# x^T U of two pairs in fp32 in four column groups, batch 1 in double pairs, and one fixed program order

## The chip, the cores and the metric

The kernel runs on one core of a Trainium2 chip. The core has five engines that work side by side and meet through semaphores: TensorE (matmul, and its weight loads), VectorE, ScalarE, GpSimd (POOL in the profile) and SyncE (SP), which here only issues DMAs. A time is the device time of one execution in microseconds; where one time is given for a kernel it is the median of its runs.

## What is computed

Linear attention, an RMS norm, and then a token-mixing and a channel-mixing layer on its output. The batch has 8 elements (called batches below), each with 8 heads, 576 positions and 64 columns a head, so x has 576 rows and 512 columns for each batch.

```python
kv = np.einsum('bhsd,bhse->bhde', k, v)
out = np.einsum('bhsd,bhde->bhse', q, kv)
rms = np.sqrt(np.mean(out * out, axis=-1, keepdims=True) + 1e-06)
attn = out / rms * g_norm                 # -> x, heads side by side
xt = x.transpose(0, 2, 1)
h = xt @ U @ V                            # U 576x32, V 32x576
u = x + h.transpose(0, 2, 1)
out = u + np.maximum(u @ w_ch1, 0.0) @ w_ch2   # 512 -> 2048 -> 512
```

## The kernel before

**Precision.** The large matmuls run in fp32r on numbers that are split in a high and a low part (hi and lo), three matmuls for each product. Small ones run in plain fp32, which TensorE does in two passes: one matmul of the program is two records in the trace.

**The channel layer.** The 8 x 576 rows of u are handled as nine blocks of 512 rows (j in the code). Blocks 0 to 2 go through `ffn1` and `ffn2` directly, 16 chunks of the 2048 columns each. Blocks 3 to 8 are taken in twos with a seven-product scheme (`product`, `product2`), whose sums and differences of u (`forms_of_u`), h (`form_of_h`) and of the weights (`sums_of_w`) VectorE and ScalarE make. The weights arrive packed and are decoded chunk by chunk during the first block (`decode_w`: a copy on ScalarE, a bit operation on VectorE, a cast on ScalarE, a subtraction on VectorE), then partly copied to DRAM (`copy_of_w`).

**The attention.** Two heads are a pair; a batch has four pairs, and two pairs are a double pair. For batches 2 to 7 a double pair is done together (`duo_tasks`): `run_step` multiplies q by K^T V for both pairs in 64-by-64 matmuls, does the tails, and in the same burst K^T V of the next double pair (`kv_double`, two column groups of 64); then squares, sums and the root (`sq`, `red`, `root`, `rms`) and the multiplications that write x (`mula`, `mulb`) follow. x is kept in `x_duo`, nine chunks of 128 columns, of which chunk 4 holds the 64 last rows of both pairs. For x^T U each pair's x is then cast to its high part (`xsplit_step`, ScalarE), the low part is made by two subtractions (`low_parts`, VectorE, into `st`), and nine fp32r matmuls of 64 weight columns (hi and lo of U side by side in `u2`) add up (`t_step`). `t4_step` builds the four-strip stationary matrix from the result, `mix_step` multiplies it by V, and `add_step` adds it to the transposed x, which takes the way of VectorE's 32-by-32 transpose and DRAM (`turn`, `out`, `in`). `into_blocks` (`g`) scales by g and splits u into its hi and lo blocks.

Batch 1 is done pair by pair instead (`pair_tasks`): an output step of five fp32 matmuls (`out_step`), x^T U in plain fp32 with 96 weight columns for pairs 0 to 2 and in the split form for pair 3 (`T32`), and K^T V as a burst of its own. Batch 0 is the start-up: it has its own steps and its own plan.

**What sets the order.** From block 0 on each step has a place, a number, in the tables (`DUOS`, `PAIRS`, `FORMSAT`, `FINISH`, `PREP`, ...). A place counts groups of twelve large matmuls: block j < 3 has places 32j to 32j + 32, one for each `ffn1` or `ffn2` chunk. `do` emits the steps whose place has been reached, between two groups of matmuls. In block 0 the emitted order binds only in part: TensorE keeps it from chunk 13 on (`PIN0`), VectorE, ScalarE and SP from place 32 on (`ORDERED`); before that a scheduler places the instructions. The q loads, the stores of the output (`finish`, with the places in `FINISH`) and the transposes' DMAs all go through SP's queue, which keeps its order.

Of the kernel before, what the change touches and what calls it, by code (L numbers as in the profile page):

```python
# [10 lines left out]
F32 = mybir.dt.float32  # L11
# [27 lines left out]
T32 = ('ffff', 'fffr')  # L39
SSQ = ('vvvv', 'vvvv', 'vvvv')  # L40
MULS = ('vvvv', 'vvvv')
STEPS = ('kv', 'kvl', 'out', 'ql', 'split', 'turn', 't', 'mix')
REST = {0: 1, 1: 47.15, 2: 77.8, 4: 113.1, 6: 167.4}
RESTLOAD = {1: 41.6, 2: 67.15, 4: 104.4, 6: 161.6}
FORMSAT = {3: ((89, 89.16, 89.27, 91.33, 91.34, 91.6, 91.61, 91.87, 92.8, 93.4, 93.85), (96, 96.26, 96.47, 97.13, 97.19, 97.95, 98.56, 99.12, 99.23, 100.54, 101.4)), 5: ((143.9, 144.21, 144.22, 147.58, 149.64, 149.8, 150.21, 151.37, 151.53, 151.95, 152.4), (149.1, 150.41, 151.97, 153.23, 153.44, 153.7, 154.56, 154.92, 155.63, 156.24, 157.3)), 7: ((194.35, 194.46, 195.47, 197.88, 200.79, 204.2, 204.31, 204.62, 204.83, 205.74, 207.4), (206.8, 207.81, 207.97, 208.58, 209.54, 209.7, 209.71, 210.17, 210.73, 211.24, 212.55))}
# [3 lines left out]
FOLLOW = {  # L49
# [22 lines left out]
PIN0 = 13  # L72
# [16 lines left out]
def build(ctx: ExitStack, tc: tile.TileContext, kv0_in, kv_in, q_in, uv_in, w_in, out):  # L89
# [20 lines left out]
    u2 = const.tile([P, NT, 2 * R], F32R, name="u2")  # L110
# [397 lines left out]
    def xsplit_step(b, p, late=False):  # L508

        s = state[b, p]  # L510
        xh = sc.tile([P, NT, P], F32R, name="xh")
        xl = st.tile([P, 4, P], F32R, name=f"st{p % 2}")
        n = p if b == 0 else -1
        move("xh", n, xh, s["x"])
        s["hl"] = (xh, xl)
        if not late:
            low_parts(s)

    def low_parts(s):

        xh, xl = s["hl"]
        n = -1
        tail = s.get("tail", 4)
        main, own = (slice(0, 4), slice(0, TAIL)) if tail else (slice(1, NT), slice(TAIL, P))
# [659 lines left out]
```

## Time and profile before

| | us |
|---|---|
| median of 3 runs (lowest, highest) | 837.23 (836.54, 837.96) |
| the profiled execution | 836.27 |
| its span | 834.5 |
| TensorE busy | 821.4 |
| VectorE busy | 590.5 |
| ScalarE busy | 362.8 |

The span is the time from the first to the last instruction of the profiled execution. Busy time is a union: a matmul's record lasts longer than its share of the stream, because matmuls are pipelined, so records overlap, and what one costs is read from the starts of its neighbours. An idle time in brackets behind a row names what ended it.

### The profile page before, as it was taken

Reading aid. Unit: us, or ns where it says so; the run is one execution under the profiler, and the core shown is the slowest. Engines: PE = TensorE matmul, PEld = TensorE weight load, DVE = VectorE, ACT = ScalarE, POOL = GpSimd, SP = SyncE. Lnnn points to the kernel's source line nnn. Section 1 sums busy time; section 2 is a strip of 40 time slices with the busy share of each in tenths; the row PEclk is TensorE's granted clock in tenths of the full one; section 3 lists DMA queues with packets and bytes.
Section 4 is the critical chain, followed back from the end, with each engine's and each line's share of the span. In section 5 each row is a group of like instructions: output and inputs, shape, how many; then the busy total and the mean of one; then the engine's idle time right before and its main releaser. Section 6 shows DMA issues by size and latency. Waiting matters only on the chain.

```text
span 834.5 us, 13626 instructions
## 1 busy us (share of the span) xinstructions
PE 821.4 (98%) x5157; PEld 681.5 (82%) x5157; DVE 590.5 (71%) x895; ACT 362.8 (43%) x615; POOL 8.3 (1%) x37
## 2 busy tenths in 40 slices
PE   8999998999999999999999999999999999999998
PEld 7788887788888788888888888888888888888886
DVE  4887655768889765849956798578557983862385
ACT  4766431333333432446535454554255445322531
POOL 3000000000000000000000000000000000000000
PEclk9999999999999999999999999999999999999999
DMA  9996767555679452879688689768667686666665
GB/s 351 382 367 245 271 235 256 184 194 166 215 218 302 154 173 85 270 258 309 223 262 272 204 273 298 258 221 239 225 182 234 209 281 196 175 201 199 198 200 176
DMA packets 109840, 195.33 MB, mean 234 GB/s; under 512 B 10832, under 2 KB 45904, under 8 KB 107984
## 3 DMA queue, kind: packets, MB, share of 16 engines
q1 hardware_dynamic: 109632, 194.33, 71.2%
q8 instruction: 41, 0.67, 0.4%
q14 instruction: 23, 0.19, 0.1%
q10 hardware_dynamic: 144, 0.13, 0.0%
HBM read 145.14 MB, written 49.28 MB: 233 GB/s over the span
## 4 chain that ended last, share of the span: by engine, by line
PE 89%; DVE 6%; ACT 2%; DMA 1%; issue 1%; SPq 0%; DVEq 0%; ACTq 0%
PE y L140 67%; PE h L140 14%; PE pt L140 4%; PE ph L140 3%; PE pp L140 3%; DVE dec L130 2%; DVE st L130 1%; DMA uvs<-uv_in 1%; DVE hhl L130 1%; DVE ss L130 1%; DVE x L130 0%; DVE h L130 0%; DMA ut<-q_in 0%; ACT hhl L130 0%; DVE ta L130 0%
## 5 line engine op out<-in xcount | busy, mean ns | idle before, releaser
L140 PE MATMUL y<-entry,ring 128*128 128x512 f32 x576 | 135.5, 390 | 0.0
L140 PE MATMUL y<-hhl,ws 128*128 128x512 f32 x540 | 132.3, 392 | 0.0
L140 PEld LDWEIGHTS y<-entry,ring 128*128 128x128 f32 x576 | 107.6, 188 | 22.3 <-DVE entry L130 0.2
L140 PE MATMUL h<-uth,ws 128*128 128x512 f32 x360 | 119.8, 393 | 0.5 <-DVE hhl L130 0.2
L140 PEld LDWEIGHTS y<-hhl,ws 128*128 128x128 f32 x540 | 99.7, 188 | 20.3 <-ACT hhl L130 0.2
L130 DVE TENSOR_TENSOR h<-y,h 128x512 f32<-128x512 f32 x71 | 48.1, 685 | 59.4 <-PE y L140 59.1
L140 PE MATMUL y<-uB,ringw 128*128 128x512 f32 x354 | 85.2, 390 | 0.0
L140 PE MATMUL y<-uT,ring 128*128 128x512 f32 x348 | 82.9, 390 | 0.0
L140 PEld LDWEIGHTS h<-uth,ws 128*128 128x128 f32 x360 | 67.6, 188 | 16.2 <-DVE hhl L130 1.7
L130 ACT ACTIVATE hhl<-h 128x512 fp32r<-128x512 f32 (+1 forms) x53 | 34.4, 648 | 101.6 <-PE h L140 86.2
L140 PEld LDWEIGHTS y<-uB,ringw 128*128 128x128 f32 x354 | 66.1, 188 | 13.8 <-issue 0.2
L140 PEld LDWEIGHTS y<-uT,ring 128*128 128x128 f32 x348 | 65.0, 188 | 13.4
L130 ACT COPY h<-y 128x512 f32<-128x512 f32 x70 | 40.6, 585 | 80.3 <-PE y L140 80.0
L130 DVE TENSOR_TENSOR entry<-h,entry 128x1024 fp32r<-128x1024 f32 x48 | 58.1, 1218 | 21.0 <-ACT entry L130 20.9
L140 PE MATMUL h<-utl,ws 128*128 128x512 f32 x180 | 70.4, 391 | 0.0
L130 DVE SCALAR_TENSOR_TENSOR hhl<-h,hhl 128x512 fp32r<-128x512 f32 (+1 forms) x53 | 39.6, 747 | 41.7 <-ACT hhl L130 41.6
L130 ACT CAST entry<-h 128x1024 fp32r<-128x1024 f32 x48 | 49.8, 1051 | 35.7 <-PE y L140 30.1
L140 PE MATMUL y<-entry,ringw 128*128 128x512 f32 x216 | 55.2, 391 | 0.0
L140 PE MATMUL y<-hhl,ringw 128*128 128x512 f32 x216 | 54.9, 390 | 0.0
L140 PE MATMUL y<-uT,ringw 128*128 128x512 f32 x210 | 50.8, 390 | 0.0
L140 PEld LDWEIGHTS y<-hhl,ringw 128*128 128x128 f32 x216 | 40.5, 188 | 8.7 <-ACT uth L130 0.3
L140 PEld LDWEIGHTS y<-entry,ringw 128*128 128x128 f32 x216 | 40.1, 188 | 8.2 <-DVE entry L130 0.2
(206 smaller groups left out, 1111.3 us busy)
## 6 DMA issues: line engine op xcount, KB each, us to landing
ring<-wd SPq DMA_DIRECT2D x69, 256.0 KB, 3.5
kv_sb<-kv_in SPq DMA_DIRECT2D x14, 1216.0 KB, 7.0
ringw<-wd SPq DMA_DIRECT2D x66, 256.0 KB, 3.4
raw<-w_in SPq DMA_DIRECT2D x30, 511.8 KB, 10.2
ring<-w1s SPq DMA_DIRECT2D x48, 256.0 KB, 3.7
ringw<-w1s SPq DMA_DIRECT2D x48, 256.0 KB, 3.5
ring<-w2s SPq DMA_DIRECT2D x48, 256.0 KB, 4.2
ringw<-w2s SPq DMA_DIRECT2D x48, 256.0 KB, 4.3
```

The source lines that it names most:

```text
L130: ins = getattr(self.eng, name)(*args, **kw)
L140: ins = nc.tensor.matmul(*args, **kw)
```

## The change

x^T U of a double pair becomes one step (`t_both`): ten fp32 matmuls take x straight from `x_duo` with 32 weight columns each, in four column groups (two halves of the sum for each pair), so that no high and low parts of x are needed. `t_sums` adds the halves (a ScalarE copy, a VectorE addition), `t4_late` builds the stationary matrix from the sum; `u1` holds U in fp32 and is filled on POOL. Batch 1 is done in double pairs like the others, with K^T V of its first one at place 6.15. Program order binds on all engines from block 0 on, and the decoding of chunks 3 to 15 gets places of its own (`DECODE`, four parts each). All tables have new numbers; of the ones cut below the numbers alone differ. Some buffers change: `xt` has one for each pair of a double pair, the forms of u and the outputs use `st0` to `st3`, and the forms of u come in another order.

```diff
-T32 = ('ffff', 'fffr')
+T32 = ('ffff',)
...
-FINISH = {0: (33.5, 34.5, 33.15, 33.3), 1: (65.55, 67.85, 66.2, 66.3), 2: (97.7, 97.85, 98.65, 101.5)}
-ORDERED = 32
+REST = {0: 8.45, 1: 50.95, 2: 85.35, 4: 113.2, 6: 160.3}
+RESTLOAD = {1: 45.05, 2: 79.45, 4: 103.6, 6: 157.7}
...
+FINISH = {0: (33.95, 37.7, 37.15, 36.75), 1: (65.96, 65.09, 66.75, 69.65), 2: (98.95, 99.85, 97.9, 100.25)}
+DECODE = ((2.36, 2.77, 2.78, 3.73), (3.34, 3.89, 4.49, 4.64), (4.45, 5.4, 5.8, 6.2), (5.41, 6.21, 7.61, 8.31), (7.07, 8.52, 9.72, 10.37), (10.38, 10.43, 10.73, 10.98), (12.4, 12.54, 12.59, 12.69), (13.4, 13.55, 13.95, 14.15), (14.26, 16.71, 16.91, 17.91), (17.27, 18.77, 20.82, 21.52), (20.98, 22.03, 22.88, 23.93), (22.39, 24.29, 25.59, 25.84), (25.35, 25.9, 26.1, 26.45))
...
-FIRSTKV = 28
-GROUPS = ('kvl', 'ql', 'run', 'sq', 'kvc', 'red', 'root', 'rms', 'mula', 'mulb', 'casta', 'suba', 'turna', 'outa', 'ina', 'ta', 't4a', 'mixa', 'adda', 'ga', 'castb', 'subb', 'turnb', 'outb', 'inb', 'tb', 't4b', 'mixb', 'addb', 'gb')
+FIRSTKV = 6.15
+GROUPS = ('kvl', 'ql', 'run', 'sq', 'kvc', 'red', 'root', 'rms', 'mula', 'mulb', 't', 'ts', 'turna', 'outa', 'ina', 'turnb', 'outb', 'inb', 't4a', 'mixa', 'adda', 'ga', 't4b', 'mixb', 'addb', 'gb')
...
-    2: ((50.5, 33.95, 35.05, 35.1, 39.55, 35.2, 35.4, 35.45, 35.55, 37.65, 36.35, 36.4, 35.8, 37.05, 38.1, 38.3, 38.6, 39.2, 40.7, 43.3, 38.55, 39.2, 38.35, 38.55, 40.4, 40.45, 41.05, 41.1, 41.3, 46.35), (32.5, 32.4, 42.6, 42.85, 52.55, 43.1, 43.25, 43.35, 43.4, 46.05, 44.75, 46.7, 46.95, 47.3, 50.25, 48.9, 51.15, 52.8, 52.9, 55, 49.75, 51.1, 51.95, 52.3, 54.15, 52, 52.1, 54.9, 55.75, 57.4)),
...
+    1: ((4.45, 10.4, 12.8, 13.2, 14.5, 13.45, 13.65, 13.75, 14.2, 14.6, 17, 18.6, 15.9, 18.85, 20, 15.55, 21.4, 24.85, 21.55, 23.3, 24.7, 25.44, 19.6, 25.1, 26.45, 26.75), (11.3, 12.9, 19.23, 19.34, 20.31, 19.65, 20.31, 20.47, 20.83, 21.92, 24.26, 25.17, 23.94, 25.75, 26.05, 22.18, 25.25, 26, 26.48, 28.09, 29.45, 31.45, 28.94, 29.85, 29.95, 31.45)),
+    2: ((14.12, 27, 31.15, 32.6, 36.4, 33.2, 33.6, 34.15, 34.85, 35.45, 39.3, 39.45, 35.5, 36.65, 38.95, 37.65, 38.9, 40.85, 39.75, 40.2, 40.6, 47.25, 40.7, 41, 42.35, 44.5), (20.95, 32.25, 43.4, 44.55, 50.15, 44.7, 45.15, 45.55, 46.05, 46.65, 48.55, 48.6, 46.8, 47.6, 49.15, 47.9, 50.95, 51.25, 50.2, 51.95, 53.05, 58.6, 48.95, 53.8, 53.85, 57.8)),
...
+    6: ((111.6, 123.1, 124.55, 124.9, 125.35, 125, 125.5, 126.25, 126.85, 127.7, 127.9, 127.95, 126.9, 127.85, 128.6, 128.5, 128.55, 130.95, 129.85, 130.9, 131.35, 135.3, 131.25, 132.75, 133.85, 144.5), (117.45, 131.7, 134.2, 134.3, 142.65, 134.4, 134.45, 134.6, 134.95, 136.45, 138.15, 138.3, 137.6, 138.35, 139.05, 137.65, 139.1, 140.35, 139.5, 140.65, 141.05, 141.55, 143.3, 144, 146.2, 149.75)),
+    7: ((125.6, 146.8, 150.65, 151, 157.05, 151.15, 152.55, 153.1, 159.5, 159.95, 160.2, 160.95, 159.65, 159.7, 163.62, 160.6, 161.2, 162.05, 161, 164.85, 165.65, 187.2, 162.6, 169.6, 172.15, 189.65), (147.3, 163.2, 176.4, 177.8, 185.85, 178.8, 179.25, 179.45, 179.9, 179.95, 180.8, 182.3, 182.35, 187.75, 188.45, 185.9, 186.55, 189.6, 186.8, 188.1, 189.75, 192.7, 189.95, 192.05, 196.1, 198.25)),
...
-LOADS = ['kv0', 'kv1', 'q1', 'uv', 'q0', 'w11', 'w10', 'q2', 'kv2', 'kv3', 'q3', 'w13', 'w12', 'w20', 'w21', 'w23', 'w22', 'kv4', 'q4']
+LOADS = ['kv0', 'kv1', 'q1', 'uv', 'q0', 'w11', 'w10', 'q2', 'kv2', 'kv3', 'q3', 'w13', 'w12', 'w20', 'w21', 'w23', 'w22', 'kv4']
...
-    u2 = const.tile([P, NT, 2 * R], F32R, name="u2")
+    u1 = const.tile([P, NT + 1, R], F32, name="u1")
+    t4s = [const.tile([P, P], F32R, name=f"t4_{k}") for k in range(2)]
...
+    def decode_parts(f):
...
+        return [top, bits, hi, low]
...
-        pp = bank()
+        pp = bank() if b == 0 else three()[1]
...
-    def xsplit_step(b, p, late=False):
...
-    def low_parts(s):
...
-            if b >= 5 and p % 2:
-                xt = wf.tile([P, 4, NT, 32], F32, name="wf")
-            else:
-                xt = sc.tile([P, 4, NT, 32], F32, name="xt")
+            xt = sc.tile([P, 4, NT, 32], F32, name=f"xt{p % 2}")
...
-        xh, xl = state[b, p]["hl"]
-        shift = NT - 1 - state[b, p].get("tail", 4)
-        todo = [(xh, i, (i + NT - shift // 4) % NT) for i in range(NT)] + [(xl, i, i) for i in range(4)]
-        for n, (xx, i, k) in enumerate(todo):
-            mm(tp[0:2 * R, 0:P], lhsT=u2[:, k, :], rhs=xx[:, i, :], start=(n == 0), stop=(n == len(todo) - 1))
+
+    def t_both(b, d):
+
+        tp = three()[1]
+        for n, row in enumerate(((0, 5, 2, 7), (1, 6, 3, 8), (4, 4))):
+            for k, c in enumerate(row):
+                own = slice(R * k, R * (k + 1))
+                u = u1[:, 4 + k if n == 2 else c % 5]
+                mm(tp[own, 0:P], lhsT=u, rhs=x_duo[:, c, :], start=(n == 0), stop=(n == (2 if k < 2 else 1)))
+
+    def t_sums(b, d):
+
+        tp = three()[1]
+        half, total = (sc.tile([2 * R, P], F32, name=name) for name in ("half", "total"))
+        act.copy(out=half, in_=tp[2 * R:4 * R, 0:P])
+        vec.tensor_tensor(out=total, in0=tp[0:2 * R, 0:P], in1=half, op=ALU.add)
+        state[b, 2 * d]["total"] = state[b, 2 * d + 1]["total"] = total
+
+    def t4_late(b, p):
+
+        a = p % 2
+        t4 = t4s[a]
+        own, total = slice(R * a, R * (a + 1)), state[b, p]["total"]
+        act.copy(out=t4[own], in_=total[own])
+        act.copy(out=t4[3 * R:], in_=total[own])
+        vec.tensor_tensor(out=t4[2 * R:3 * R], in0=total[own], in1=t4[own].bitcast(F32), op=ALU.subtract)
+        state[b, p]["t4"] = t4
...
-        if b < 2:
-            for lo in (0, n):
-                mp = bank()[:, 0:n]
-                mm(mp, lhsT=t4, rhs=v4[:, lo:lo + n], start=True, stop=True)
-                own = ut32[p][:, lo:lo + n]
-                vec.tensor_tensor(out=own, in0=mp, in1=own, op=ALU.add)
-        else:
-            for k in range(2):
-                mm(three()[0][:, k, 0:n], lhsT=t4, rhs=v4[:, k * n:(k + 1) * n], start=True, stop=True)
-            return
-        into_blocks(b, p)
+        for k in range(2):
+            mm(three()[0][:, k, 0:n], lhsT=t4, rhs=v4[:, k * n:(k + 1) * n], start=True, stop=True)
...
-            outs = [st.tile([P, DM], F32, name=f"st{c}") for c in range(3)] + [ldp.tile([P, S], F32, name="q_sb")[:, 0:BLK]]
+            outs = [st.tile([P, DM], F32, name=f"st{c}") for c in range(3)] + [st.tile([P, DM], F32, name="st3")]
...
-            if name == "T4":
-                t[name] = t["T2"]
-            else:
-                t[name] = st.tile([P, BLK], F32, name="st2") if name == "T2" else ldp.tile([P, S], F32, name="q_sb")[:, 0:BLK]
+            t[name] = t["T1"] if name in ("T2", "T4") else st.tile([P, BLK], F32, name=f"st{2 * i + int(name == 'T3')}")
...
-        move("u", 0, u2[:, :, 0:R], uvv)
-        minus("u", 1, u2[:, :, R:], uvv, u2[:, :, 0:R].bitcast(F32))
+        nc.gpsimd.tensor_copy(out=u1[:, 0:4], in_=uvv[:, 0:4])
+        for k in range(2):
+            own = slice(TAIL * k, TAIL * (k + 1))
+            nc.gpsimd.tensor_copy(out=u1[own, 4 + k], in_=uvv[own, 4])
...
-    def pair_tasks(b, p, places):
...
-            steps = dict(cast=lambda p=p: xsplit_step(b, p, True), sub=lambda p=p: low_parts(state[b, p]), turn=lambda p=p: turn_step(b, p, True),
-                         out=lambda p=p: out_of_xt(b, p, state[b, p]["xt"]), t=lambda p=p: t_step(b, p), t4=lambda p=p: t4_step(b, p),
+            steps = dict(turn=lambda p=p: turn_step(b, p, True), out=lambda p=p: out_of_xt(b, p, state[b, p]["xt"]), t4=lambda p=p: t4_late(b, p),
                          mix=lambda p=p: mix_step(b, p), add=lambda p=p: add_step(b, p), g=lambda p=p: into_blocks(b, p))
...
+        at(places["t"], lambda: t_both(b, d))
+        at(places["ts"], lambda: t_sums(b, d))
...
-    at(FIRSTKV, lambda: kv_step(2, 0))
+    at(FIRSTKV, lambda: kv_step(1, 0))
...
+    for f, places in enumerate(DECODE, NF - len(DECODE)):
+        for place, what in zip(places, decode_parts(f)):
+            at(place, what)
...
+    ordered[0] = pinned[0] = True
...
-            pinned[0] = j > 0 or f >= PIN0
-            if j == 0:
-                while ahead < min(NF, f + 1 + AHEAD):
-                    decode_w(ahead)
-                    ahead += 1
...
-            ordered[0] = 32 * j + 2 * f >= ORDERED
```

## Rows read from the trace of the kernel before

**Rows 1.** The page, part 1: busy us (share of span) x instructions of each engine.
```profile
PE 821.4 (98%) x5157; PEld 681.5 (82%) x5157; DVE 590.5 (71%) x895; ACT 362.8 (43%) x615; POOL 8.3 (1%) x37
```

**Rows 2.** Busy time by stretch: stretch, its length, each engine, clock, DMA share, GB/s.
```profile
160.00:340.00 180.00, 179.13 (x1345) 148.01 (x1344) 138.98 (x251) 68.84 (x141) 0.00 (x0) 1.00 0.61 195
```

**Rows 3.** TensorE's timeline, one pair of batch 7: start, us, operation, count.
```profile
485.26 1.52 PE L140 MATMUL y<-hhl,ringw 128*128 128x512 f32 x6
486.62 0.46 PE L140 MATMUL pt<-xh,u 128*64 128x128 f32 x5
486.92 0.40 PE L140 MATMUL pt<-st,u 128*64 128x128 f32 x4
487.15 1.58 PE L140 MATMUL y<-entry,ringw 128*128 128x512 f32 x6
488.57 1.52 PE L140 MATMUL y<-hhl,ringw 128*128 128x512 f32 x6
```

**Rows 4.** TensorE's timeline, a burst of K^T V alone in block 0.
```profile
122.78 1.39 PE L140 MATMUL pp<-kv_sb 128*64 128x64 f32 x40
124.10 3.02 PE L140 MATMUL y<-hhl,ws 128*128 128x512 f32 x12
126.95 0.43 PE L140 MATMUL pp<-v,t 128*128 128x288 f32 x2
```

**Rows 5.** TensorE's timeline, a run step: output, tails, next K^T V.
```profile
364.30 1.52 PE L140 MATMUL y<-uB,ring 128*128 128x512 f32 x6
365.75 1.16 PE L140 MATMUL ph<-kvb,ut 64*64 64x64 f32 x64
366.85 0.44 PE L140 MATMUL pt<-kvb,ut 128*64 128x128 f32 x4
367.11 1.33 PE L140 MATMUL pt<-kv_sb 128*64 128x64 f32 x40
368.38 1.66 PE L140 MATMUL y<-uB,ring 128*128 128x512 f32 x6
```

**Rows 6.** TensorE's timeline, batch 1: an output step, then a plain x^T U.
```profile
105.64 1.27 PE L140 MATMUL pp<-kvb,q_sb 128*128 128x128 f32 x10
106.75 1.25 PE L140 MATMUL pp<-xh,wf 128*96 128x128 f32 x10
107.76 0.47 PE L140 MATMUL h<-uth,ws 128*128 128x512 f32 x1
```

**Rows 7.** The list of waits, TensorE: us in total, times, longest us.
```profile
PE pt L140 <- DVE st L130: 1.4, 4, 0.5
```

**Rows 8.** TensorE's timeline, the first of those waits.
```profile
229.31 0.46 PE L140 MATMUL pt<-xh,u 128*64 128x128 f32 x5
230.07 0.45 PE L140 MATMUL pt<-st,u 128*64 128x128 f32 x4 [0.30 <-DVE st L130]
```

**Rows 9.** TensorE's timeline, the start of batch 2.
```profile
140.87 2.88 PE L140 MATMUL y<-hhl,w2s 128*128 128x512 f32 x12
147.13 1.58 PE L140 MATMUL ph<-kvb,ut 64*64 64x64 f32 x64 [3.38 <-DMA ut<-q_in]
...
151.40 0.50 PE L140 MATMUL h<-uth,ws 128*128 128x512 f32 x1
```

**Rows 10.** Busy time by stretch, columns as in rows 2.
```profile
146.77:160.00 13.23, 12.87 (x147) 10.89 (x148) 8.88 (x18) 3.00 (x6) 0.00 (x0) 0.87 0.49 143
```

**Rows 11.** The SP queue's timeline at that place.
```profile
143.64 0.33 SPq L130 DMA_DIRECT2D out<-st  x1
144.02 0.92 SPq L130 DMA_DIRECT2D ut<-q_in  x2
```

**Rows 12.** Groups by shape, ScalarE: count, busy us, mean ns, idle before and releaser.
```profile
L130 ACT CAST t<-pt 64x128 fp32r<-64x128 f32 x24 | 6.1, 254 | 15.2 <-PE pt L140 15.2
```

**Rows 13.** Groups by shape, TensorE's weight loads, columns as in rows 12.
```profile
L140 PEld LDWEIGHTS y<-uT,ringw 128*128 128x128 f32 x210 | 39.3, 188 | 8.1
...
L140 PEld LDWEIGHTS pt<-xh,u 128*64 128x64 f32 x120 | 10.8, 135 | 3.1
```

More of the change, by code (lines that the diff above doesn't have):

```diff
@@ L55 @@
 SB_AT = {3: 96, 5: 152, 7: 208}
-PAIRS = {
-    1: ((4, 8, 6, 3, 6, 11, 10, 16), (10, 10, 11, 8, 11, 12, 14, 21), (14, 17, 16, 13, 16, 19, 20, 26), (17, 20, 19, 16, 20, 22, 24, 29)),
-}
-FIRSTKV = 28
-GROUPS = ('kvl', 'ql', 'run', 'sq', 'kvc', 'red', 'root', 'rms', 'mula', 'mulb', 'casta', 'suba', 'turna', 'outa', 'ina', 'ta', 't4a', 'mixa', 'adda', 'ga', 'castb', 'subb', 'turnb', 'outb', 'inb', 'tb', 't4b', 'mixb', 'addb', 'gb')
-DUOS = {
[6 rows of a table removed]
+FIRSTKV = 6.15
+GROUPS = ('kvl', 'ql', 'run', 'sq', 'kvc', 'red', 'root', 'rms', 'mula', 'mulb', 't', 'ts', 'turna', 'outa', 'ina', 'turnb', 'outb', 'inb', 't4a', 'mixa', 'adda', 'ga', 't4b', 'mixb', 'addb', 'gb')
+DUOS = {
[7 rows of a table added]
 }
@@ L71 @@
 G0 = 2 * NT * P + 1
-PIN0 = 13
 HALF = NF // 2
@@ L270, in decode_w, with top, bits, hi @@
         whole[f] = w
+    def decode_parts(f):
+        t = {}
+        def top():
+            raw = raws[f].rearrange("p w c -> p (w c)")
+            act.copy(out=tops.bitcast(FP16).rearrange("p (n t) -> p n t", t=2)[:, :, 1],
+                     in_=raw.bitcast(BF16).rearrange("p (n t) -> p n t", t=4)[:, :, 2])
+        def bits():
+            raw = raws.pop(f).rearrange("p w c -> p (w c)")
+            t["tmp"] = dec_tile(1)
+            vec.scalar_tensor_tensor(out=t["tmp"].bitcast(U32), in0=raw.bitcast(U32).rearrange("p (n t) -> p n t", t=2)[:, :, 0],
+                                     scalar=13, in1=tops.bitcast(U32), op0=ALU.logical_shift_right, op1=ALU.bitwise_or)
+        def hi():
+            t["w"] = weight_slot(f"ws{f}", [P, 4, 2, DM // 2], F32R, f)
+            act.copy(out=t["w"][:, :, 0], in_=t["tmp"].rearrange("p (a c) -> p a c", a=4))
+        def low():
+            w = t["w"]
+            vec.tensor_tensor(out=w[:, :, 1], in0=t["tmp"].rearrange("p (a c) -> p a c", a=4), in1=w[:, :, 0].bitcast(F32), op=ALU.subtract)
+            for n, which in enumerate(("w1", "w2")):
+                keep(which, f, w[:, 2 * n:2 * n + 2])
+            whole[f] = w
+        return [top, bits, hi, low]
     def to_dram(name, src):
@@ L506, in mul_step @@
                                 in1=rv[0:TAIL, 4].unsqueeze(2).broadcast_to([TAIL, 2, D]), op=ALU.mult)
-    def xsplit_step(b, p, late=False):
[L510 to L517, printed above, removed]
-    def low_parts(s):
[L521 to L524, printed above, removed]
-        other = slice(TAIL, P) if tail else slice(0, TAIL)
-        vec.tensor_tensor(out=xh[other, tail], in0=s["x"][own, tail], in1=xh[own, tail].bitcast(F32), op=ALU.subtract)
-        minus("xl", n, xl, s["x"][:, main], xh[:, main].bitcast(F32))
     def turn_step(b, p, late=False):
@@ L567, in t_step @@
             return
-        xh, xl = state[b, p]["hl"]
-        shift = NT - 1 - state[b, p].get("tail", 4)
-        todo = [(xh, i, (i + NT - shift // 4) % NT) for i in range(NT)] + [(xl, i, i) for i in range(4)]
-        for n, (xx, i, k) in enumerate(todo):
-            mm(tp[0:2 * R, 0:P], lhsT=u2[:, k, :], rhs=xx[:, i, :], start=(n == 0), stop=(n == len(todo) - 1))
+    def t_both(b, d):
[19 more added lines that the diff above has]
+        state[b, p]["t4"] = t4
     def t4_step(b, p):
         tp = state[b, p]["tp"]
-        t4 = t40[p] if b == 0 and p in t40 else sc.tile([P, P], F32R, name=f"t4_{p % 2 if b > 1 else 0}")
+        t4 = t40[p]
         low = slice(2 * R, 3 * R)
@@ L748, in less @@
         def less(name, in0, in1):
-            if name == "T4":
-                t[name] = t["T2"]
-            else:
-                t[name] = st.tile([P, BLK], F32, name="st2") if name == "T2" else ldp.tile([P, S], F32, name="q_sb")[:, 0:BLK]
+            t[name] = t["T1"] if name in ("T2", "T4") else st.tile([P, BLK], F32, name=f"st{2 * i + int(name == 'T3')}")
             vec.tensor_tensor(out=t[name], in0=value(in0), in1=value(in1), op=ALU.subtract)
-        return [lambda: parts("B11"), lambda: parts("B21"), lambda: less("T1", "B12", "B11"), lambda: less("T2", "B22", "T1"),
-                lambda: parts("T2"), lambda: parts("T1"), lambda: less("T4", "B21", "T2"), lambda: less("T3", "B22", "B12"),
-                lambda: parts("T3"), lambda: parts("B22"), lambda: parts("T4")]
+        return [lambda: parts("B11"), lambda: parts("B21"), lambda: less("T1", "B12", "B11"), lambda: parts("T1"),
+                lambda: less("T2", "B22", "T1"), lambda: parts("T2"), lambda: less("T4", "B21", "T2"), lambda: parts("T4"),
+                lambda: less("T3", "B22", "B12"), lambda: parts("T3"), lambda: parts("B22")]
     loaded = {}
@@ L867, in build @@
     nc.gpsimd.memset(u0[:, :, R:2 * R], 0.0)
+    nc.gpsimd.memset(u1[:, 4:6], 0.0)
+    for t in t4s:
+        nc.gpsimd.memset(t.bitcast(F32), 0.0)
     for t in x0:
@@ L873, in build @@
     make_identity(nc, ident)
-    t40 = {p: st.tile([P, P], F32R, name=f"st{p - 1}") for p in (1, 2, 3)}
+    t40 = {p: st.tile([P, P], F32R, name=f"st{(p - 1) % 4}") for p in range(NPAIR)}
     early = [temps[:, i * DM:(i + 1) * DM] for i in range(2)]
@@ L886, in build @@
         "kv4": lambda: load_kv(1, 0),
-        "q4": lambda: load_q(1, 0),
     }
@@ L917, in build @@
     tasks = [(PLAN["uv"], uv_step), (PLAN["v4"], v4_step), (PLAN["g"], g_step)]
-    ahead = 1 + len(PLAN["d"])
     for f, place in enumerate(PLAN["d"]):
@@ L931, in build @@
     tasks.append((PLAN["x0"], lambda: decode_first("w2", early[1], 2)))
-    def next_load(load, b, p):
-        nxt = (b, p + 1) if p + 1 < NPAIR else (b + 1, 0)
-        if nxt[0] < 2 or load is load_kv and nxt[0] < 3:
-            load(*nxt)
-    def split_step(b, p):
-        if not plain(b, p):
-            xsplit_step(b, p)
-    attention = dict(kv=kv_step, out=out_step, stats=stats_step, mul=mul_step, split=split_step, turn=turn_step,
-                     t=t_step, t4=t4_step)
     for _, what in sorted(tasks, key=lambda t: t[0]):
@@ L959, in do @@
                 what()
-    def pair_tasks(b, p, places):
-        def run(*names):
-            for name in names:
-                attention[name](b, p)
-        def o():
-            run("out", "stats", "mul", *([] if plain(b, p) else ["turn"]))
-        def t():
-            run("t", "t4")
-        for name, what in (("kv", lambda: run("kv")), ("kvl", lambda: next_load(load_kv, b, p + 1) if p % 2 == 0 else None), ("out", o),
-                           ("ql", lambda: next_load(load_q, b, p)), ("split", lambda: run("split")), ("turn", lambda: run("turn") if plain(b, p) else None), ("t", t), ("mix", lambda: mix_step(b, p))):
-            at(places[name], what)
     def duo_tasks(b, d, places):
@@ L981, in duo_tasks @@
         late = {}
-        at(places["kvl"], lambda: load_kv(b, 2 * d) if (b, d) > (2, 0) else None)
+        at(places["kvl"], lambda: load_kv(b, 2 * d) if (b, d) > (1, 0) else None)
         at(places["ql"], lambda: [dma(ut32[p], q_in[b, p]) for p in pairs])
@@ L1025, in build @@
         rest_of(h, b)
-    for b, bases in PAIRS.items():
-        for p, places in enumerate(bases):
-            pair_tasks(b, p, dict(zip(STEPS, places)))
-    at(FIRSTKV, lambda: kv_step(2, 0))
+    at(FIRSTKV, lambda: kv_step(1, 0))
     for b, duos in DUOS.items():
@@ L1052, in build @@
         at(h, lambda n=n: copy_of_w(n))
-    at(33, lambda: copy_of_w(NF - 1))
     for j in range(NSTD):
```

10 lines of the change are left out of this document (3 added, 7 removed), and 14 rows, old and new, of tables (DUOS, FOLLOW).

## The prediction

> **What bounds the kernel now.** I read the page's first part before anything else: TensorE counts as busy for 821.4 us of a span of 834.5 [rows 1]. A busy TensorE can still be waiting inside its pipeline, so the next view is the table by stretch. From 160 to 340 us, a stretch with much work for VectorE, TensorE is busy for 179.13 of 180 us, VectorE for 139 and ScalarE for 69 [rows 2]. No other engine is at its limit there. So a change is worth what it takes out of TensorE's own stream, or out of the few places where that stream stops. The third view is TensorE's timeline: there a group of small matmuls is priced by how far it pushes the large ones apart. Six large matmuls (512 columns) take 1.36 us, 0.227 each [rows 3]; all prices below are start to start against that pitch. The fourth view, the list of waits, names the stops.
>
> **x^T U in batches 2 to 7.** Now each pair does nine matmuls with 64 weight columns and 128 moving columns in fp32r. From the first of them (486.62) to the end of the next six large ones (488.57) it is 1.95 us; less 1.36 that is 0.59 us a pair [rows 3], and 24 pairs cost 14.2 us. The change does two pairs at once: ten fp32 matmuls of 32 weight columns in four column groups. An fp32 matmul is two recorded instructions, so that is 20, in six waves if four run side by side (three rows of the loop, two passes each; the third row fills two groups only).
>
> This shape is not in the trace. The nearest is the K^T V burst, also fp32 and over all 128 rows, in two column groups: 40 instructions from 122.78 to 124.10, with the twelve large ones behind it 0.13 late (124.10 to 126.95 against 2.72) [rows 4] and 0.09 before it (365.75 instead of 364.30 + 1.36 = 365.66) [rows 5], 1.54 us in all. Its 40 instructions proper take 1.27 us in 20 waves (367.11 to 368.38), so entering and leaving cost 0.27. A wave of 128 columns costs between 0.101 (ten such fp32 instructions one after the other in 1.01 us, 106.75 to 107.76) [rows 6] and 0.13 (the four of the tails, two at a time, in 0.26, 366.85 to 367.11) [rows 5]. Six waves and 0.27 make 0.88 to 1.05 us for two pairs; I take 1.0, close to the two-group rows. If the burst got in and out as cheaply as today's (0.59 less nine at half of 0.101 leaves 0.14), it would be 0.75. If the column groups did not run side by side at all, it would be 20 x 0.101 + 0.27 = 2.29. Term: 12 x 1.0 - 14.2 = **-2.2 us**.
>
> **Waits inside these bursts.** TensorE waited four times for the low part of x, which VectorE writes into st [rows 7]. At 229.31 the five matmuls on the high part are followed by the next at 230.07, 0.76 later instead of 0.30 (486.62 to 486.92), so 0.46 late [rows 3, 8]. That cast and subtraction are gone. Term: 4 x 0.46 = **-1.8 us**.
>
> **Batch 1 in double pairs.** Now it costs TensorE four output steps of 1.11 us (105.64 to 106.75), three fp32 x^T U of 1.01 and one of 0.59, and three K^T V bursts of 1.54 (two for batch 1, one for batch 2) [rows 3, 4, 6]: 4.4 + 3.6 + 4.6 = 12.7 us. Afterwards: one K^T V burst alone, 1.54; two run steps, each with the next K^T V in it, 2.72 (365.66 to 368.38) and 0.13 behind it, 2.85 each [rows 5]; and two of the new x^T U, 2.0. Together 9.2. The mix matmuls are eight on either side. Term: **-3.4 us**.
>
> **The stop at the start of batch 2.** The twelve large matmuls from 140.87 end at 143.59, and the run step starts at 147.13, 3.45 us later than it could after the usual 0.09; released by a q load. The step itself then takes 4.27 us (147.13 to 151.40) instead of 2.63: behind those 3.5 idle us the mean granted clock from 146.77 to 160 is 0.87, part of it at the lower of the two levels [rows 5, 9, 10]. Together 5.1 us lost. The load was issued at 144.02, right behind an output store on the same SP queue [rows 11]. The numbers in the code say why: q at place 33.95, run at 35.05, and the stores of block 0 from 33.15 to 34.5, each behind a sum on VectorE. A place is twelve large matmuls, 2.72 us. Afterwards q stands at 27, ahead of the stores (33.95 and later), and run at 31.15: 11.3 us ahead. Term: **-5.1 us**. Next late at this point would be the copies of K^T V (kvc), which the order puts right before.
>
> **What is hidden.** VectorE loses two subtractions for each pair and ScalarE one cast. They gain, for two pairs, one copy out of PSUM of the kind that takes 0.25 us [rows 12] and one addition of the same size; the two copies and the subtraction for t4 stay. All of this lies beside the large matmuls, between x^T U and the mix, and VectorE has 41 of 180 us free in its fullest stretch [rows 2]; if that cover were gone, each such copy would show with its 0.25. On POOL two small clears and three copies of U replace one subtraction before block 0. Three moved edits I cost at nothing: the weight decode at fixed places in block 0 (each chunk two or more places, 5.4 us, ahead of its first matmul), the other order of the forms of u, and the loads and copies to DRAM on the SP queue. Each is bounded by the stop they could make, the 5.1 us above, and below by the 0.87 us that TensorE idles from 160 to 340 [rows 2].
>
> **What is added in waits.** With program order on all engines from block 0 on, an instruction that waits holds all behind it on its engine; on TensorE that is the large matmuls. The tightest spots in the new numbers are batch 6 and batch 7, first double pair: the new x^T U stands 0.2 and 0.25 of a place behind the multiplication that writes its x (127.9 behind 127.7, 160.2 behind 159.95). The nearest row for such a wait is the 0.46 above; two make **+1.0 us** rounded up.
>
> **A rule of the Trainium skill against the change.** In the K^T V burst two column groups share all rows, and 40 instructions with their 40 weight loads pass in 1.27 us [rows 5], so loads of 64 columns are hidden there; nothing shows four groups with loads of 32. A load takes 188 ns for 128 columns and 135 for 64 [rows 13], so 32 columns are worth 26.5 ns. The Trainium skill's page "TensorE: Matmul & The Clock Gate", section "Part 3: Packing small matmuls — row/col tiling", says that a weight load overlaps a running matmul only where its row group is another one, and these four groups share theirs. By that rule the 40 loads in rows 5 should have shown; they did not, so the trace so far speaks against it, and I keep it as a rival: 833.1 by the rule, worked out below, 825.7 by the row.
>
> **Sum.** -2.2 - 1.8 - 3.4 - 5.1 + 1.0 = -11.5 us. The profiled execution took 836.27 us (span 834.5), which gives 824.8; the median of the three runs is 837.23, 1.0 above it, and gives **825.7 us**.
>
> **Rivals.**
> A wait takes the stop's place: q for batch 1 is issued 2.4 places (6.5 us) ahead of its run step, at 10.4 against 12.8, right after the last loads of raw weights; a load needs 3.1 us from issue (144.02 to 147.13), so it should be in time. If not, one stop of 5.1 returns: 830.8. Chance 0.10.
> The loads show: 20 loads of 26.5 ns are 0.53 us for each of 14 double pairs, 7.4 us: 833.1. Chance 0.08.
> The other side, slower, where the change doesn't do what it says: the four groups run one after the other. Then x^T U costs 2.29 instead of 1.0, 14 x 1.29 = 18.1 us more: 843.8. The point from which this decides is a burst of 1.82 us, where the 11.5 are used up. For it: no row shows more than two column groups. Against it: two groups halve the time in rows 5, and the 64-by-64 burst there passes 64 instructions in 1.10 us, four tiles at a time. Chance 0.08.
> Better than forecast: bursts at 0.75 (-3.5), no new waits (-1.0), and the idle time of rows 2 gone with the lighter VectorE (-0.9): 820.3. Chance 0.06.
>
> **How the numbers follow.** The forecast itself has 0.68; its own bounds (0.75 to 1.05 a burst, no wait to three more of 0.46) give 821 to 828. The range reaches to the better case and to the loads that show, 818 to 834, and leaves out the serial groups and small tails of the rest. What can be told from no change is 0.2%, 1.7 us. Faster: 0.68 + 0.10 + 0.08 + 0.06 = 0.92, of which I move 0.03 to no change, for two of these mishaps at once: 0.89, 0.03, and 0.08 slower.
>
> **What would show it.** The new burst pushes the large matmuls apart by 1.0 us (0.88 to 1.05; 1.5 if loads show, 2.3 if serial). No wait on st and no wait for q near 144 us in the list of waits. Batch 1 shows two bursts of 64 in place of four output steps. VectorE's busy time falls by the subtractions on x while TensorE's idle time stays within 1 us of today's. The forecast is wrong if TensorE's large matmuls stop in block 0, where the fixed order is new.

## The result and the profile after

The changed kernel takes 826.67 us (median of 4 runs, 825.56 to 828.49) against 837.60 for the kernel before in the same session: ratio 0.9874, 95% interval 0.9852 to 0.9895, so it is faster by 10.9 us. The forecast was 825.7. The execution that the profile shows is the longest of the four, 828.49 us with a span of 826.7; against the profiled execution of before that is 7.8 us, and the ledger further down is made for these two traces.

The page, part 1, after (busy us, share of the span, instructions), beside [rows 1]:

```profile
PE 815.4 (99%) x5278; PEld 671.4 (81%) x5278; DVE 564.6 (68%) x842; ACT 353.2 (43%) x600; POOL 8.5 (1%) x41
```

VectorE lost 25.9 us of work, ScalarE 9.6, and neither was the bound. TensorE is still the engine that has no room, with 121 more instructions and 6.0 us less busy time. Its list of waits after (us in all, times, longest):

```profile
PE pp L136 <- ACT w1s L126: 2.9, 1, 2.9
PE h L136 <- DVE eps L126: 1.1, 1, 1.1
PE pp L136 <- DVE x L126: 0.9, 2, 0.6
PE h L136 <- DVE hhl L126: 0.8, 2, 0.4
...
PE ph L136 <- DVE ut L126: 0.5, 1, 0.5
```

The waits for st of [rows 7] and the wait for q of [rows 9] are gone. A new one leads the list, 2.9 us for w1s, the decoded first-layer weights of chunk 0. Three stretches of TensorE's timeline after: the start of block 0, which no row of before showed; a double pair's x^T U in batch 1, which answers to [rows 3]; and the run step at the start of batch 2, at 134.18 now, which answers to [rows 9].

```profile
31.63 0.52 PE L136 MATMUL pp<-v,st 128*128 128x256 f32 x3
35.09 0.80 PE L136 MATMUL pp<-uth,w1s 128*128 128x512 f32 x1 [2.94 <-ACT w1s L126]
35.68 0.63 PE L136 MATMUL pp<-utl,w1s 128*128 128x512 f32 x1
...
40.46 0.63 PE L136 MATMUL h<-uth,ws 128*128 128x512 f32 x1
...
41.32 0.64 PE L136 MATMUL h<-uth,ws 128*128 128x512 f32 x2
...
87.14 2.88 PE L136 MATMUL y<-hhl,ws 128*128 128x512 f32 x12
89.95 0.85 PE L136 MATMUL pt<-x,u 128*32 128x128 f32 x20
90.73 0.50 PE L136 MATMUL h<-uth,ws 128*128 128x512 f32 x1
...
134.18 1.16 PE L136 MATMUL ph<-kvb,ut 64*64 64x64 f32 x64
135.27 0.44 PE L136 MATMUL pt<-kvb,ut 128*64 128x128 f32 x4
135.54 1.33 PE L136 MATMUL pt<-kv_sb 128*64 128x64 f32 x40
136.80 0.50 PE L136 MATMUL h<-uth,w1s 128*128 128x512 f32 x1
```

At the usual pitch of 0.227 us, every second large matmul starts 0.45 us later. Here it is 0.86 us (40.46 to 41.32). The table by stretch says why (columns as in [rows 2]; the last three are the granted clock, the DMA share and GB/s):

```profile
28.00:35.09 7.09, 4.15 (x31) 3.51 (x29) 6.87 (x10) 5.65 (x12) 0.00 (x0) 0.96 1.03 408
35.09:41.50 6.41, 6.41 (x15) 4.86 (x16) 2.35 (x5) 0.60 (x1) 0.61 (x1) 0.51 0.53 173
41.50:60.00 18.50, 18.41 (x114) 14.79 (x114) 9.66 (x10) 10.17 (x12) 0.00 (x0) 1.00 1.01 400
```

Behind the idle 2.94 us the mean granted clock is 0.51 for 6.4 us, so nearly all of that stretch runs at the lower of the two levels (1.2 GHz). In that stretch TensorE counts as busy for 6.41 of 6.41 us and does half the work: the busy share alone hides this loss.

What TensorE waits for is a chain of work on VectorE and ScalarE. ScalarE's and VectorE's timelines at that place:

```profile
32.93 0.33 ACT L126 ACTIVATE ut<-pp,g_sb 128x64 f32<-128x64 f32 x1
34.41 0.62 ACT L126 CAST w1s<-temps 128x512 fp32r<-128x512 f32 x1 [1.16 <-DVE temps L126]
```

```profile
32.57 1.22 DVE L126 TENSOR_TENSOR ws<-dec,ws 128x1024 fp32r<-128x1024 f32 x1
33.70 0.68 DVE L126 SCALAR_TENSOR_TENSOR temps<-w1raw,dec 128x512 uint32<-128x512 uint32 x1
```

The cast of chunk 0's w1 waits for VectorE's temps, and that stands behind the 1.22 us subtraction for chunk 2's weights (chunk 1's was done by 29 us). Before, the cast came as late (34.57), but TensorE stood for only 0.2 us at a time: its order there was free, and it took the first-layer matmuls of chunk 1, the first of them at 30.38, and then a K^T V of batch 1. TensorE's timeline of before:

```profile
30.38 0.50 PE L140 MATMUL h<-uth,ws 128*128 128x512 f32 x1
...
35.91 1.39 PE L140 MATMUL pp<-kv_sb 128*64 128x64 f32 x40
```

**The ledger of the two traces** (7.8 us), each burst priced by how far it pushes the large matmuls apart:

```
start of block 0                        +5.1
batch 1 (14.37 -> 10.38 us, mixes in)   -4.0
run step at the start of batch 2        -5.1   (7.92 -> 2.83)
x^T U, batches 2 to 7 (16.7 -> 12.2)    -4.5   (old waits for st in the 16.7)
other waits, old and new                +0.7
```

The first line is worked out at the 60th large matmul: it starts 2.41 us later than before, though a K^T V burst (1.53) and an output step (1.13) that used to lie ahead of it now lie behind it. The ledger accounts for 7.8 us; the other 3.1 us by which the medians differ lie in executions that have no trace.

### The profile page after: what moved, and what is told of

Read it like the earlier page. It is cut to its first block, busy times and chain, and to the rows that moved or that the text cites. A ratio compares the mean times of both kernels' runs of the same rounds, so it can differ in the third digit from the quotient of the medians.

```text
span 826.7 us, 13787 instructions
## 1 busy us (share of the span) xinstructions
PE 815.4 (99%) x5278; PEld 671.4 (81%) x5278; DVE 564.6 (68%) x842; ACT 353.2 (43%) x600; POOL 8.5 (1%) x41
## 4 chain that ended last, share of the span: by engine, by line
PE 83%; DMA 4%; DVE 3%; SPq 1%; ACT 1%; issue 1%; DVEq 0%; ACTq 0%
PE y L136 64%; PE h L136 13%; PE pt L136 3%; PE ph L136 3%; SPq L126 1%; DMA ut<-xt 1%; DMA xt<-xt 1%; DMA ring<-w2s 1%; DVE dec L126 1%; DMA ut<-q_in 1%; DVE h L126 0%; DMA ringw<-wd 0%; DVE xt L126 0%; ACT hhl L126 0%; DVE entry L126 0%
## 5 line engine op out<-in xcount | busy, mean ns | idle before, releaser
L136 PEld LDWEIGHTS y<-hhl,ws 128*128 128x128 f32 x540 | 100.3, 188 | 21.3 <-ACT hhl L126 0.6
L126 ACT ACTIVATE hhl<-h 128x512 fp32r<-128x512 f32 (+1 forms) x53 | 34.4, 649 | 116.8 <-PE h L136 113.1
L126 DVE TENSOR_TENSOR entry<-h,entry 128x1024 fp32r<-128x1024 f32 x48 | 58.2, 1218 | 26.0 <-ACT entry L126 25.9
```

The lines of the kernel that those rows point to most:

```text
L126: ins = getattr(self.eng, name)(*args, **kw)
L136: ins = nc.tensor.matmul(*args, **kw)
```

## The experiments

The sessions of the experiments gave the kernel before 838.2 to 838.9 us, against 837.6 in the session of the result. So a difference of about 1 us between an experiment and the changed kernel's 826.67 us says nothing by itself. No experiment takes batch 1 alone; its -4.0 rests on the ledger.

**1. The stop alone.** The kernel before, with one number changed: the place of batch 2's first q load.

```diff
-    2: ((50.5, 33.95, 35.05, ...
+    2: ((50.5, 32.3, 35.05, ...
```

> The kernel before with one number changed: the q load of batch 2's first double pair at place 32.3, ahead of block 0's output stores, instead of 33.95 behind them. Theory (the change's gain is TensorE's stream, term by term): the stop of 3.45 us at the start of batch 2 and the slow run step behind it go, 5.1 us, so 832.5 against 837.6. Rival (TensorE stops there anyway, for the store's sum on VectorE or the next copy): within 1 us of before, 836.6 to 838.

Measured: 833.75 us (832.62 to 834.48), ratio 0.9944 (0.9922 to 0.9966), 4.5 us faster. TensorE's timeline of this kernel, the run step in question:

```profile
144.32 1.16 PE L140 MATMUL ph<-kvb,ut 64*64 64x64 f32 x64
145.41 0.44 PE L140 MATMUL pt<-kvb,ut 128*64 128x128 f32 x4
145.68 1.33 PE L140 MATMUL pt<-kv_sb 128*64 128x64 f32 x40
```

No wait, and the step passes in the usual time. So the stop was a q load issued too late, its price was the idle time and the half-clock stretch behind it, and one number gets most of it back without the rest of the change: 4.5 of the 5.1 us by the medians. Next late, and new, is a wait of 1.3 us for the activated hidden block, 7 us behind the step.

**2. The new x^T U alone, in the kernel before.** Two runs. In the first the burst stands behind the place of mulb, which the numbers of before set late; in the second mulb is moved right behind mula, so that x is final.

```diff
+        places["mulb"] = places["mula"] + .05      # second run only
+        places["t"] = max(places["ta"], places["mulb"] + .05)
+        places["ts"] = places["t"] + .02
...
-    ... cast=xsplit_step, sub=low_parts, t=t_step, t4=t4_step
+    ... t4=t4_late; at(places["t"], t_both); at(places["ts"], t_sums)
```

> The kernel before with the new x^T U (one burst of ten fp32 matmuls in four column groups for two pairs) in batches 2 to 7 alone; batch 1 and all orders stay, but for pair 3 of batch 1, which takes the plain form (0.5 us more on TensorE) to make room. Theory: 12 bursts of 0.98 in place of 24 of 0.59 give 2.4 us, the four waits for st another 2.2, less 0.5: 833.5 against 837.6. Rival (what counts is the work taken from VectorE and ScalarE, 1.7 and 1.2 us a double pair): more than 6 us, below 831.5.

> The kernel before with the new x^T U in batches 2 to 7 alone, as in b_t_both, and with the place of mulb put right behind that of mula, so that x of both pairs is final ahead of the burst. Theory (the burst is worth some 4 us wherever x is ready for it; b_t_both lost because its bursts stood behind x): the start-up order that came with the edit costs the same 3.6 us as in b_t_both, the stop at the start of batch 2 (7.9 us for a step of 2.8) stays, the twelve bursts give 4 to 4.5 us back: 837.5 us, between 835 and 840. No burst waits for x by more than 0.3 us. Rival (in the rest of the kernel before, DVE has no room for mulb so early, and other steps go late instead): above 842 us, with waits of TensorE for DVE in the run steps of batches 2 to 5.

Measured: 847.68 us (846.56 to 850.6), ratio 1.0117 (1.0089 to 1.0144), and 845.71 us (841.36 to 847.36), ratio 1.0084 (1.0058 to 1.011). Both are slower than before, and both forecasts missed. TensorE's timeline of the first, one burst:

```profile
293.61 0.41 PE L141 MATMUL pt<-x,u 128*32 128x128 f32 x2
296.60 1.49 PE L141 MATMUL pt<-x,u 128*32 128x128 f32 x18 [2.59 <-DVE x L131]
298.02 5.22 PE L141 MATMUL y<-hhl,ws 128*128 128x512 f32 x12
```

Two matmuls start, eighteen wait 2.59 us for x, and the twelve large ones behind them take 5.2 us instead of 2.9. In the second run all twelve bursts pass in 0.98 us each, as in the changed kernel, and the waits have moved on to the mix and the run steps. TensorE's waits of the second run, and behind them VectorE's timeline at the longest of these waits:

```profile
PE ph L141 <- DVE ut L131: 4.3, 2, 3.0
PE ph L141 <- DMA ut<-q_in: 4.2, 2, 3.4
```

```profile
281.57 0.76 DVE L131 TENSOR_TENSOR ut<-ph,ut 128x576 f32<-128x576 f32 x1 [4.85 <-DMA ut<-xt]
```

The rival's time held (above 842), and other steps did go late, but its reason is not what the trace shows. The 4.3 us are two mixes that wait for VectorE, and VectorE itself stood idle for 4.85 us there, until a DMA brought the transposed x; the run steps wait for q loads, 3.4 us of it at the old stop. So at these places it was not VectorE's room that was short; DMAs came late, and why was not followed.

Both runs also lose 3.6 and 4.2 us by the 60th large matmul. Their start-up, which the scheduler orders, came out in another order than before; which of the added steps does that was not followed. What follows: the burst costs what it was priced at wherever it does not wait, but it needs x of both pairs at one time, and with the places of before, moved only this far, the edit gains nothing. The -4.5 of the ledger belong to the burst and the numbers together.

**3. How the column groups run.** The changed kernel with the ten matmuls in another order (two groups at a time; group after group), and with all in one column group. In that last one the sums of the two pairs fall together in the same 32 rows of PSUM, so it no longer computes x^T U of each pair.

```diff
-        for n, row in enumerate(rows):
-            for k, c in enumerate(row):
+        for ks in ((0, 2), (1, 3)):                # or ((0,), (1,), (2,), (3,))
+            for n, row in enumerate(rows):
+                for k in [k for k in ks if k < len(row)]:
...
-                own = slice(R * k, R * (k + 1))
+                own = slice(0, R)                  # the third run alone
```

> The changed kernel with the same twenty matmul instructions of x^T U in another order: first pair a (two column groups), then pair b (the other two), so twelve waves of two in place of six waves of four. Theory (side by side in four groups, 0.109 us a wave): six waves more, 0.65 us in each of 14 bursts, 9.2 us: 835.9 against 826.7. Rival (the groups do not matter, VectorE's and ScalarE's lighter load made the gain): within 1 us of the changed kernel, 825.7 to 827.7.

> The changed kernel with x^T U's matmuls ordered group by group, so that none run side by side: twenty waves. Theory: 14 waves more of 0.109 us, 1.53 us in each of 14 bursts, 21.4 us: 848 against 826.7, slower than before. Rival: within 1 us of the changed kernel.

> The changed kernel with all ten matmuls of x^T U in one column group, into the same 32 rows of PSUM, so that none can run beside another; the sum is that of both pairs mixed and the other rows are left over, so the output is not the reference's. Theory (price of the burst is its waves of 0.109 us and 0.27): 20 waves, 2.45 instead of 0.98 us in each of 14 bursts, 20.6 us: 847 against 826.7, slower than before. Rival (the burst's price does not reach the end): below 833.

Measured: two at a time 831.29 us (830.46 to 833.55; 0.992, 0.9894 to 0.9945), group after group 830.31 (830.12 to 830.98; 0.9903, 0.9879 to 0.9927), one group 848.32 (847.49 to 850.44; 1.0105, 1.0081 to 1.0129). The forecast of the third held (847). The second missed by 18 us, and the first by 4.6, with its rival missing as well. TensorE's timelines of the three in that order, the first burst of each with its neighbours:

```profile
90.76 2.88 PE L136 MATMUL y<-hhl,ws 128*128 128x512 f32 x12
93.57 1.09 PE L136 MATMUL pt<-x,u 128*32 128x128 f32 x20
94.59 0.50 PE L136 MATMUL h<-uth,ws 128*128 128x512 f32 x1
```

```profile
87.86 2.88 PE L136 MATMUL y<-hhl,ws 128*128 128x512 f32 x12
90.67 1.13 PE L136 MATMUL pt<-x,u 128*32 128x128 f32 x20
91.74 0.50 PE L136 MATMUL h<-uth,ws 128*128 128x512 f32 x1
```

```profile
89.77 2.88 PE L136 MATMUL y<-hhl,ws 128*128 128x512 f32 x12
92.58 2.37 PE L136 MATMUL pt<-x,u 128*32 128x128 f32 x20
94.88 0.50 PE L136 MATMUL h<-uth,ws 128*128 128x512 f32 x1
```

From the first of the twenty to the next large matmul it is 0.78 us in the changed kernel, 1.02, 1.07 and 2.30 in these. Pushed apart: 0.98, 1.24, 1.27 and 2.52 us. Twenty in one group are 0.115 us each, one after the other; 14 x (2.52 - 0.98) = 21.6 us, and the time differs from the changed kernel's by 21.7. That is the rival of serial groups, run on purpose: it would have made the change a loss. The written order of the groups costs only 0.26 to 0.29 us a burst, since even group after group most of the work overlaps. The grouping decides here, not the order. (In one group the ten matmuls also add into the same rows; the two can't be told apart by this edit.)

All three traces have one more wait that the changed kernel's trace has not. TensorE's waits of the first:

```profile
PE pt L136 <- DMA kv_sb<-kv_in: 2.1, 1, 2.1
```

It is 2.1, 1.5 and 2.1 us in the three, at about 76 us. The first edited burst comes later, at 90 us, so the order of the burst can't be its cause. It is the K and V load of batch 1's second double pair. In the changed kernel that load is issued at 67.25 and lands 7.2 to 7.4 us later, at most 0.4 us before its first matmul at 74.86; in the first of the three it takes 9.8 us. In the first and the third the clock drops behind this wait, and with that it sets the large matmuls back by some 3.7 us; some other waits are shorter there than in the changed kernel. So the agreement of 21.6 and 21.7 is closer than the parts are: in the traces the bursts are 21.3 of 22.0 us. Why the load takes longer in some executions was not followed.

**4. The start of block 0.** The changed kernel with chunk 1's first-layer matmuls written ahead of chunk 0's; the same with K^T V of batch 1 in the gap as well; the first again, but with chunk 1's last three matmuls behind chunk 0's instead; and the changed kernel with the fixed order of ScalarE, VectorE and TensorE undone in block 0. The matmuls written ahead stand before the line that fixes the order, so the scheduler still places them among the start-up's.

```diff
+    h1 = ps_h.tile([P, BLK], F32, name="h")
+    ffn1(h1, 1, range(ND), 0)                      # a_chunk1_last: range(ND - 1), the rest in block 0
     for d in range(ND - 1):
...
-FIRSTKV = 6.15
+FIRSTKV = 1.5                                      # a_chunk1_kv alone
...
-    ordered[0] = pinned[0] = True                  # a_free_block0 alone: from chunk 13 and block 1 on
```

> The changed kernel with the twelve ffn1 matmuls of chunk 1 emitted ahead of chunk 0's, so that they lie where TensorE now waits 2.94 us for the cast of w1's chunk 0. Theory (the fixed order costs some 5 us at the start of block 0, because TensorE can no longer take chunk 1 first; 2.9 as a wait and the rest at the lower clock behind it): the wait and the slow matmuls go, but ffn2 of chunk 0 then follows its relu with nothing between, 1.3 us or so: 822.5 against 826.7. Rival (the start is bound by the decoding on VectorE and ScalarE, whatever TensorE does first): within 1 us of the changed kernel, 825.7 to 827.7.

> As a_chunk1_first, and K^T V of batch 1's first double pair at place 1.5 instead of 6.15, in a PSUM bank of the start-up, so that its 1.5 us cover the relu of chunk 0. Theory: 1.3 us better than a_chunk1_first, 821.2. Rival: within 0.7 us of a_chunk1_first.

> a_chunk1_first with the last three of chunk 1's twelve first-layer matmuls in block 0 (those of the fourth slice of x) moved behind chunk 0's last one. In a_chunk1_first TensorE waits there 0.78 and 0.16 us for chunk 0's activated halves. Theory (what is left of the loss at the start of block 0 is a want of independent matmuls, and 0.7 us of them can stand in that wait): the wait at 39.3 falls to under 0.3 us, some of it comes back as a wait for ACT's cast of w1 at 35, sum 0.3 to 0.9 us less than a_chunk1_first: 822.4 us, between 821.5 and 823.5. Rival (the earlier wait for w1 takes it all back, and TensorE stops longer there): the same as a_chunk1_first or slower, 823 to 825.5 us.

> The changed kernel with the fixed order undone in block 0, as the kernel before has it: TensorE bound from chunk 13, the other engines from place 32; all places stay. Theory: the scheduler again takes chunk 1 first and the start gets back what the fixed order costs it, 4 to 5 us, if nothing else in block 0 gets worse: 822.5. Rival (the fixed order is itself part of the gain, since the scheduler's model puts decoding and relus in the wrong order): slower than the changed kernel, 828 or more.

Measured: 822.95 us (822.84 to 825.05; ratio 0.9812, 0.979 to 0.9834), 824.39 (824.01 to 825.66; 0.9826, 0.9805 to 0.9846), 823.0 (822.79 to 824.75; 0.9822, 0.9792 to 0.9853) and 824.56 (824.27 to 825.41; 0.9827, 0.9807 to 0.9846). The first forecast holds, and that kernel beats the ones before and after the change: its interval and the changed kernel's don't touch. TensorE's timeline of the first, at the place where the changed kernel stands:

```profile
33.63 0.39 PE L136 MATMUL h<-uth,ws 128*128 128x512 f32 x1
34.23 0.51 PE L136 MATMUL h<-uth,ws 128*128 128x512 f32 x1 [0.21 <-ACT uth L126]
35.01 0.51 PE L136 MATMUL h<-utl,ws 128*128 128x512 f32 x1 [0.28 <-DVE utl L126]
...
35.59 0.40 PE L136 MATMUL pp<-uth,w1s 128*128 128x512 f32 x1
...
39.30 0.47 PE L136 MATMUL y<-hhl,w2s 128*128 128x512 f32 x1 [0.78 <-ACT hhl L126]
39.93 2.79 PE L136 MATMUL y<-hhl,w2s 128*128 128x512 f32 x11 [0.16 <-DVE hhl L126]
```

Twelve matmuls whose weights were ready fill the wait, w1s is there when its turn comes, and the large ones stand at the usual pitch: clock 1.00 from 20 to 40 us, 0.86 in the changed kernel. By the 60th large matmul 3.8 of the 5.1 us are back.

The other three can't be told from it by their intervals; their traces show why they are no better. K^T V at 1.5 fills the 0.78 us at 39.30, but it had been the filler of another gap. TensorE's timeline of that kernel, and its table of that stretch:

```profile
50.73 2.88 PE L136 MATMUL y<-hhl,ws 128*128 128x512 f32 x12
55.56 0.50 PE L136 MATMUL h<-uth,ws 128*128 128x512 f32 x1 [1.94 <-DVE hhl L126]
```

```profile
50.00:60.00 10.00, 8.06 (x29) 6.17 (x29) 4.96 (x5) 4.79 (x5) 0.00 (x0) 0.85 1.03 412
```

A stop of 1.94 us, and the clock falls behind it. With chunk 1's last three matmuls moved, the gap at 39 is filled and the wait for w1s is back ahead of it. TensorE's timeline:

```profile
35.00 0.50 PE L136 MATMUL pp<-uth,w1s 128*128 128x512 f32 x1 [0.92 <-ACT w1s L126]
...
38.45 0.39 PE L136 MATMUL h<-uth,ws 128*128 128x512 f32 x1
```

Its time, 823.0, lies in the range of the theory and of the rival; the trace is the rival's, for what the later gap gains the earlier wait takes back. The forecast of the second, 1.3 us better than the first, did not come either. The kernel with a free order in block 0 regains the start as the first one does. From TensorE's waits of that kernel:

```profile
PE pp L136 <- ACT w1s L126: 0.2, 1, 0.2
```

Its clock is 1.00 from 20 to 60 us. So on this stretch the fixed order as written costs, and one moved step is about as good as the scheduler's order there.

## Why the prediction was right, and where it was not

The time came out 1.0 us above the forecast, and the size is right partly by luck. One loss of 5.1 us was not foreseen, and the other terms were together only 1.4 us better than their price. In the two traces the forecast's 11.5 us are therefore 3.7 too many; the medians hide most of that, for a reason that no trace shows.

- **What bounds the kernel**: right. In the ledger the 7.8 us are TensorE's stream and its stops, and the 35.5 us of work that VectorE and ScalarE lost need no term of their own.
- **x^T U, -2.2, and the waits inside, -1.8**: the burst was priced at 1.0 and takes 0.98, 0.78 from its first matmul to the next large one and 0.20 for entering and leaving. The records start in six waves, as said, 0.09 to 0.13 us apart. But counting waves does not price other orders: two groups at a time should have cost 0.65 more and cost 0.26. Ten of the twelve bursts cost 0.98, two have a wait of 0.2. Together -4.5 for the forecast's -4.0; the old waits cost 2.5 rather than 1.8.
- **Batch 1, -3.4**: -4.0 in the ledger. The two run steps cost 2.83 each and the single K^T V burst 1.52, as priced from [rows 4, 5]; the old batch 1 was dearer than summed.
- **The stop, -5.1**: right to the tenth in the trace, and experiment 1 shows the cause by itself. The q load is issued at 123.21 now, 11.0 us ahead of its run step, and that is enough.
- **New waits, +1.0 at the bursts of batches 6 and 7**: near in size (+0.7), but by luck: of the two bursts named, batch 7's shows no wait and batch 6's is 0.2 us late, and the largest of the small new waits is 0.5 us for ut ahead of the run step at 269.90.
- **The start of block 0, which has no term**: this is the step that failed. The section on added waits saw that program order makes a waiting instruction hold all behind it, but looked for tight spots among the new places alone, and found those of batches 6 and 7. The cover of two places or more was said of each chunk's decode; it holds for the chunks that have places, from 3 on. Chunk 0's decode has no such room: its w1 comes off VectorE at 34.4 and ScalarE at 35.0. What covered it before was TensorE's free choice among ready matmuls, and the change took that away. By the prediction's own sign (large matmuls that stop in block 0) it is wrong there. The loss is 5.1 us net, as large as the bound that the prediction gave to such a stop: 2.94 idle and some 3.0 at half clock (35.09 to 41.32 for fourteen pitches, 3.2 at full clock), less 0.9 by which the rest of that stretch is shorter than before. Experiment 4 gets 3.8 of it back with one moved step.
- **Rivals**: serial groups and loads that show are both refuted. The price of the first was too low: 2.29 us a burst and 843.8 forecast, 2.52 and 848.3 when forced, since an instruction takes 0.115 rather than 0.101. A wait as long as the old stop did come, at block 0, not at batch 1's q. At batch 1 it is the K and V load, and not q, that is close to late (experiment 3).

On the loads: in the changed kernel four groups share all their rows, each of the twenty instructions has a weight load of its own (0.110 us for 32 columns, 2.2 us in all), and all twenty pass in 0.78 us. The Trainium skill's page "TensorE: Matmul & The Clock Gate", section "Part 3: Packing small matmuls — row/col tiling", says in its list of what overlaps that a load does so only where the row group is another; by that the twenty loads would have shown. The trace disagrees, as [rows 5] did. Another sentence of that section also lets a load go ahead into a background weight buffer, which would fit; no run here tests that.

The traces differ by 7.8 us and the medians by 10.9, because the profiled execution of the changed kernel was 1.8 us above its median and that of before 1.3 below its own. Which stretch makes the 3 us between the changed kernel's own runs is open: only the longest has a trace, and the wait for kv_sb of experiment 3 is not in it.

## What to carry to other kernels

Small fp32 matmuls with 32 weight columns were worth packing in four column groups here (0.98 us a burst against 2.52 in one): the written order mattered little, the groups did. Before fixing program order on an engine, list for each of its stalls in the free order which later work filled them; that work must be written ahead of the stall, or the stall comes back, and with it a stretch at the lower clock that the busy share doesn't show. A faster step that needs its inputs all at one time can be a loss until the steps around it have new places. And a forecast that comes out in the sum can still have a large term missing: the ledger of two traces shows it, the time does not.

## What was not expected of the hardware

- Matmuls written column group by column group still overlap: 1.07 us for twenty where one group takes 2.30, and 0.78 written in turns.
- An idle time of 2.94 us was followed by 6.4 us at a granted clock of 0.51; one of 1.94 us by a stretch of ten with a mean of 0.85. Idle times of 0.78 and 0.92 us were followed by none that shows: in those two kernels the clock is 1.00 from 30 to 44 us and from 34 to 44 us.
